# Per-head maximum and minimum subtracted ahead of two exponentials in a gated linear-attention and gMLP kernel

## The chip, the cores and the metric

The kernel runs on one core of a Trainium2 chip. The metric is the device time of one execution in microseconds. A core has five engines that work side by side, each through its own instructions in order: TensorE (PE, matmuls, with its weight loads shown as PEld), VectorE (DVE), ScalarE (ACT), GpSimd (POOL) and SyncE (SP, which here only issues DMAs). They wait for each other by semaphores.

## The reference

Two branches work on the same input `x` (2048 rows of 512 numbers) and are mixed by a gate of each row.

```python
q, k, v = heads of x @ wqkv                      # 32 heads of 16
pq, pk = q @ w_phi, k @ w_phi                    # per head, 16x16
phi_q = concat(softmax(pq), softmax(-pq))        # over the 16 of a head
phi_k = concat(softmax(pk), softmax(-pk))
kv = phi_k^T @ v ;  z = sum over rows of phi_k   # per head
a = ((phi_q @ kv) / (phi_q @ z + 1e-06)) @ wo
zz = gelu(x @ w_in) ; z1, z2 = halves, z2 layer-normalised
b = (z1 * (w_sp @ z2 + b_sp)) @ w_out
out = g * a + (1 - g) * b                        # g = sigmoid(x . gate_w)
```

The change concerns the four softmaxes: a softmax is the exponentials of 16 numbers divided by their sum, and it stays the same when one number is subtracted from all 16 beforehand.

## The kernel before, in words

The 2048 rows are 16 tiles of 128 rows (one row per partition). `xT` holds x transposed, and all weights lie in SBUF. PSUM is one tile `ps` of eight banks of 512 fp32. The order of the work is written out by hand: the scheduler is off (`tc.manual_schedule()`), so each engine gets its instructions in the order in which the program issues them, and the framework adds only the waits.

The program has three stages:

- **First stage (lines 471 to 514).** `z_piece` multiplies x by `w_in`, `z_post` applies gelu, and `bn_stats` (L224) and `ln_batch` normalise; `z1_gate` (L272) scales z1. `v_proj` (L279) makes v and `fold` (L299) multiplies the weights of q and k with `w_phi`, so that p comes out of one matmul group. At its end come `k_proj(0)`, `k_proj(1)` and then the last five `z1_gate`.
- **Key stage (lines 528 to 542).** For each tile i: `gg(1)` makes half a tile of `w_sp @ z2` (16 matmuls, L405), with the eight `kv_mm` (L377) of tile i-2 between its last matmuls; then `k_norm(i)`, then `k_proj(i+2)`. At i = 7, 9 and 11 a `q_proj` is added, and one step later another `gg(1)` and the `q_norm` that goes with it. After the loop come `q_proj(3)`, two `gg` halves, `kv_acc(15)` and `kv_extract`, which copies the masked kv out of PSUM into `kvx` (L388, L393).
- **Query stage (lines 543 to 560).** For each tile j: none to two `gg` halves (`gg_at`) with the `q_mm` (L427) of tile j, `q_num(j)` (L431: a reciprocal of the denominators and one multiply on VectorE, then a transposing DMA), `q_proj(j+4)`, `q_norm(j+3)`, and `out_tile(j-3)` (L445: ten matmuls, an eviction by ScalarE and the output's DMA, which ScalarE's queue issues).

Both `k_proj` and `q_proj` do four matmuls of 512 columns (L326) into a bank of their own pair (`KBANK`, `QBANK`) and call `feat_exp` (L331). It reads that bank twice on ScalarE: exp(p) and exp(-p), written as bf16 into a slot `e` (pieces of `w_in`, and once of `xn`, whose first content is no longer needed). `norm` (L336) then sums each 16 on VectorE (L339), takes the reciprocals (L341), and multiplies: VectorE the first half of the features, GpSimd the second (L343). `q_norm` also transposes the slot by a DMA (L371) for `q_mm`.

Each `gg` half is finished on VectorE by the step "u" (L413), which adds the bias and multiplies by z1.

Of the kernel before, what the change touches and what calls it, by code (L numbers as in the profile page):

```python
# [7 lines left out]
AF = mybir.ActivationFunctionType  # L8
ALU = mybir.AluOpType
AX = mybir.AxisListType  # L10
FP32 = mybir.dt.float32
# [3 lines left out]
P = 128  # L15
S = 2048
D = 512
H = 32
DH = 16
# [10 lines left out]
DEN_EPS = 1e-6  # L30
NHG = 8
HW = 4 * DH
# [7 lines left out]
def kernel(  # L40
# [14 lines left out]
    nc = tc.nc  # L55
# [3 lines left out]
    pers = ctx.enter_context(tc.tile_pool(name="pers", bufs=1))  # L59
    ring2 = ctx.enter_context(tc.tile_pool(name="ring2", bufs=2))  # L60
# [4 lines left out]
    ps = psp.tile([P, 8, CH], FP32, name="ps")  # L65

    def zbank(t):
# [18 lines left out]
    wphi = pers.tile([P, NDT, P], BF16, name="wphi")  # L86
    mask16 = pers.tile([P, 8], BF16, name="mask16")
    mask4 = pers.tile([P, 4], BF16, name="mask4")
    xn = pers.tile([P, 2, D], BF16, name="xn")
    ones = nc.const_aps.tensor(1.0, [P, P], BF16)  # L90
    stats = pers.tile([P, NT, 2, 6], FP32, name="stats")
# [11 lines left out]
        out=ident[:], in_=ident[:], pattern=[[-1, P]],  # L103
# [14 lines left out]
    for d0 in (0, 2):  # L118
# [6 lines left out]
        out=wv[:, :, :],  # L125
        in_=A_wqkv[:, 2 * D:3 * D].rearrange("(dt p) n -> p dt n", p=P),
    )
    for q in range(1, NCH):
        nc.sync.dma_start_transpose(
            out=xT[:, :, q * CH:(q + 1) * CH], in_=x2[q * CH:(q + 1) * CH, :]  # L130
        )
        if q == 1:
            nc.sync.dma_start(
                out=wphiW[:, :, :],
                in_=A_w_phi.rearrange("(g h) e f -> (h e) g f", g=NDT),
# [3 lines left out]
        out=bcolb[:, :, :], in_=B_b_sp.rearrange("(t p) -> t p", p=P)  # L139
# [7 lines left out]
    for t in range(WSLOTS):  # L147
        load_wsp(t)
    nc.sync.dma_start(
        out=w_out[:, 0:NFT - 1, :],  # L150
        in_=B_w_out[0:(NFT - 1) * P, :].rearrange("(ft p) n -> p ft n", p=P),
# [4 lines left out]
        out=w_out[0:last_m, NFT - 1, :], in_=B_w_out[(NFT - 1) * P:FH, :]  # L156
    )
    nc.sync.dma_start(
        out=wo[:, :, :], in_=A_wo.rearrange("(g p) n -> p g n", p=P)
# [4 lines left out]
        out=mask16[:], in_=mask16[:], pattern=[[-16, 8]],  # L164
# [3 lines left out]
        out=mask16[:], in_=mask16[:], pattern=[[16, 8]],  # L168
# [3 lines left out]
    for u in upad:  # L172
        nc.gpsimd.memset(u[:, FH:FPAD], 0.0)
    nc.gpsimd.memset(vv[:, :, :, HW:VP], 1.0)
    nc.vector.tensor_tensor(out=mask4[:], in0=mask16[:, 0:4], in1=mask16[:, 4:8], op=ALU.add)

    def z_piece(t, n0, n1, d0=0, d1=NDT):
# [136 lines left out]
    ek_t = {}  # L314
# [3 lines left out]
    def e_slot(i):  # L318
        if i == 5:
            flat = xn[:].rearrange("p t d -> p (t d)")  # L320
        else:
            flat = w_in_flat[:, i * 2 * D:(i + 1) * 2 * D]
        return flat.rearrange("p (g a n) -> p g a n", g=NHG, a=2)

    def feat_mm(t, w, b, dt):
        nc.tensor.matmul(  # L326
            ps[:, b, :], lhsT=xT[:, dt, t * P:(t + 1) * P], rhs=w[:, dt, :],
            start=(dt == 0), stop=(dt == NDT - 1),
        )

    def feat_exp(b, e):  # L331
        src = ps[:, b, :].rearrange("p (g n) -> p g n", g=NHG)
        for a, sc in enumerate((1.0, -1.0)):
            nc.scalar.activation(out=e[:, :, a, :], in_=src, func=AF.Exp, scale=sc)  # L334

    def norm(e):  # L336
        ev = e.rearrange("p g a (h f) -> p (g a h) f", h=4)
        zs = ring2.tile([P, 2 * H], FP32, name="zs")
        nc.vector.tensor_reduce(out=zs[:], in_=ev, axis=AX.X, op=ALU.add)  # L339
        rs = ring2.tile([P, 2 * H], FP32, name="rs")  # L340
        nc.vector.reciprocal(out=rs[:], in_=zs[:])  # L341
        for eng, sl in ((nc.gpsimd, slice(H, 2 * H)), (nc.vector, slice(0, H))):
            eng.tensor_tensor(  # L343
                out=ev[:, sl, :], in0=ev[:, sl, :],
                in1=rs[:, sl, None].to_broadcast([P, H, DH]), op=ALU.mult,
            )

    def k_proj(t):
        ek_t[t] = e_slot(t % 4)
        b = KBANK[t % 2]  # L350
        for dt in range(NDT):
            feat_mm(t, wk, b, dt)
        feat_exp(b, ek_t[t])

    def k_norm(t):
        norm(ek_t[t])

    def q_proj(t):
        eq_t[t] = e_slot(4 + t % 2 if t < 4 else (t - 4) % 6)
        b = QBANK[t % 2]  # L360
        for dt in range(NDT):
            feat_mm(t, wq, b, dt)
        feat_exp(b, eq_t[t])
# [2 lines left out]

    def q_norm(t):
        e = eq_t.pop(t)
        norm(e)
        eT = wqkT[:, 2 * (t % 4):2 * (t % 4) + 2, :].rearrange("p a (b n) -> p (a b) n", n=P)  # L370
        nc.sync.dma_start_transpose(out=eT, in_=e.rearrange("p g a n -> p (g a n)"))  # L371
        eT_t[t] = eT
# [14 lines left out]
    def kv_extract():  # L387
        nc.vector.tensor_tensor(  # L388
            out=kvx[:, :, 0:HW].rearrange("p g (h d) -> p g h d", h=4),
            in0=slots[:, :, 0:HW].rearrange("p g (h d) -> p g h d", h=4),  # L390
            in1=mask4[:, None, :, None].to_broadcast([P, NHG, 4, DH]), op=ALU.mult,
        )
        nc.vector.scalar_tensor_tensor(  # L393
            out=kvx[:, :, HW:QW], in0=slots[:, :, HW:HW + 1].to_broadcast([P, NHG, 4]),
            scalar=0.5 * DEN_EPS, in1=mask4[:, None, :].to_broadcast([P, NHG, 4]),
            op0=ALU.add, op1=ALU.mult,
        )

# [110 lines left out]
    for t in range(NT - VLAG, NT):  # L509
        v_proj(t)  # L510
    k_proj(0)
    k_proj(1)
    for t in range(NT - 5, NT):
        z1_gate(t)
# [13 lines left out]
    for i in range(NT):  # L528
        gg(1, kv_short(i - 2) if i >= 2 else ())
        k_norm(i)  # L530
        if i + 2 < NT:
            k_proj(i + 2)
        if i in Q_AT:
            q_proj(Q_AT[i])
        if i - 1 in Q_AT:
            gg(1)
            q_norm(Q_AT[i - 1])

    q_proj(3)
    gg(2, kv_short(NT - 2))  # L540
    kv_acc(NT - 1)
    kv_extract()
    gg_at = {0: 1, 1: 1, 2: 2, 3: 1, 5: 1, 7: 1, 9: 1, 11: 1, 13: 1, 14: 1}
    for j in range(NT):
        short = [lambda g=g: q_mm(j, g) for g in range(NHG)]
        if 0 < j and j in gg_at:
            gg(gg_at[j], short)
        else:
            gg(gg_at.get(j, 0))
            for mm in short:  # L550
                mm()
        q_num(j)
        if j + 4 < NT:
            q_proj(j + 4)
        if j + 3 < NT:
            q_norm(j + 3)
        if j >= LAG:
            out_tile(j - LAG)
# [30 lines left out]
```

## Time and profile before

| | |
|---|---|
| time, median of 3 runs | 207.92 us (207.85 to 208.15) |
| the profiled execution's own time | 208.12 us |
| its span in the profile | 206.4 us |
| busy: PE, PEld, DVE | 202.3, 117.8, 148.5 us |
| busy: ACT, POOL | 82.1, 49.5 us |
| granted TensorE clock | 1.00 |
| one feature tile on ACT (L334) | 2 x 596 ns |
| its sums, reciprocals, multiply on DVE (L339, L341, L343) | 1209, 553, 693 ns |
| its multiply on POOL (L343) | 1475 ns |
| "u" on DVE (L413) | 574 ns |
| 128x512 evictions from PSUM on ACT (L286, L457) | 603, 597 ns |

The span runs from the first to the last instruction of the profile; the rest of an execution's time lies around it. A row of a group gives its line, its engine, what it writes and reads with the shapes, the number of instructions, then their busy time and the mean of one, then the idle time of the engine just before them and what ended most of it. In a timeline the first number is the start and the second the length in microseconds, and a bracket holds the idle time before with the instruction that ended it.

### The profile page before, as it was taken

To read this page: it belongs to the slowest core of one execution; us is meant where nothing else is said; L and a number is where in the kernel's file an instruction comes from. 1 tells how busy PE (TensorE), PEld (TensorE's weight loads), DVE (VectorE), ACT (ScalarE), POOL (GpSimd) and SP (SyncE) were. 2 spreads that over 40 slices of the span, in tenths; PEclk is the share of its full clock that TensorE was granted. 3 is DMA by queue.
4 is the path that set the end of the run, shared out by engine and by line. 5 is a ranking of instruction groups with operands and counts; after the bars stand their busy time and mean duration, and the time that the engine had idled before them with its cause. 6 is when DMAs were issued, how large, how long until landed. Compare 5 with 4: busy or idle time off the path is not lost.

```text
span 206.4 us, 3685 instructions
## 1 busy us (share of the span) xinstructions
PE 202.3 (98%) x1399; PEld 117.8 (57%) x1399; DVE 148.5 (72%) x304; ACT 82.1 (40%) x145; POOL 49.5 (24%) x46
## 2 busy tenths in 40 slices
PE   8999999999999999999999999999999999999994
PEld 8545555554455666666666667666455555555542
DVE  1049858385887888879898996798989788796500
ACT  4266767675684324250505102222524243341122
POOL 4000000000002353525352543032532252322000
PEclk9999999999999999999999999999999999999999
DMA  5999899997000638463757781145756974566451
GB/s 160 289 178 247 189 170 226 168 192 231 0 3 0 140 65 117 102 112 85 153 126 109 139 174 41 38 91 84 161 131 122 127 176 98 129 141 153 110 110 51
DMA packets 90378, 26.50 MB, mean 128 GB/s; under 512 B 84296, under 2 KB 90360, under 8 KB 90360
## 3 DMA queue, kind: packets, MB, share of 16 engines
q1 hardware_dynamic: 87360, 23.87, 60.2%
q10 hardware_dynamic: 3000, 2.39, 3.8%
q8 instruction: 11, 0.18, 0.4%
q14 instruction: 7, 0.06, 0.1%
HBM read 3.44 MB, written 2.10 MB: 27 GB/s over the span
## 4 chain that ended last, share of the span: by engine, by line
PE 96%; DMA 2%; SPq 0%; ACT 0%; issue 0%
PE ps L405 36%; PE ps L180 18%; PE ps L326 13%; PE ps L448 10%; PE ps L453 7%; PE ps L282 7%; DMA w_in<-in_B_w_in_dram 2%; PE ps L427 2%; PE ps L377 2%; PE ps L305 1%; SPq L112 0%; SPq L108 0%; ACT ob L457 0%; PE ps L209 0%
## 5 line engine op out<-in xcount | busy, mean ns | idle before, releaser
L405 PE MATMUL ps<-zz,wsp 128*128 128x344 bf16 x512 | 84.1, 309 | 0.0
L343 POOL TENSOR_TENSOR w_in<-w_in,rs 128x512 bf16<-128x512 bf16 x28 | 41.3, 1475 | 124.7 <-DVE rs L341 112.4
L405 PEld LDWEIGHTS <-wsp 128*128 128x128 bf16 x512 | 49.9, 98 | 28.1
L334 ACT ACTIVATE w_in<-ps 128x512 bf16<-128x512 f32 x56 | 30.1, 596 | 63.3 <-issue 21.4
L180 PE MATMUL ps<-w_in,xT 128*128 128x512 bf16 (+2 forms) x200 | 39.7, 350 | 0.4 <-DMA w_in<-in_B_w_in_dram 0.4
L339 DVE TENSOR_REDUCE zs<-w_in 128x64 f32<-128x1024 bf16 x28 | 33.8, 1209 | 0.0
L413 DVE SCALAR_TENSOR_TENSOR u<-ps,bcol,zz 128x344 bf16<-128x344 f32 x32 | 18.4, 574 | 18.6 <-PE ps L427 8.3
L180 PEld LDWEIGHTS <-xT 128*128 128x128 bf16 x200 | 19.1, 98 | 18.0 <-issue 0.8
L215 ACT ACTIVATE zz<-ps 128x1376 bf16<-128x1376 f32 (+2 forms) x18 | 21.4, 1190 | 18.6 <-PE ps L180 18.6
L448 PE MATMUL ps<-w_out,uT 128*128 128x512 bf16 (+2 forms) x102 | 23.5, 366 | 0.0
L224 DVE BATCH_NORM_STATS2 stats<-zz 128x6 f32<-128x344 bf16 x32 | 14.8, 505 | 11.1 <-ACT zz L215 11.1
L377 PE MATMUL ps<-vv,w_in 128*128 128x65 bf16 x128 | 21.7, 193 | 0.0
L343 DVE TENSOR_TENSOR w_in<-w_in,rs 128x512 bf16<-128x512 bf16 x28 | 19.4, 693 | 1.0
L341 DVE RECIPROCAL rs<-zs 128x64 f32<-128x64 f32 x32 | 17.7, 553 | 3.2
L457 ACT ACTIVATE ob<-ps 128x512 bf16<-128x512 f32 (+2 forms) x17 | 9.7, 572 | 25.1 <-PE ps L453 19.9
L453 PE MATMUL ps<-wo,oT 128*128 128x512 bf16 (+2 forms) x68 | 16.6, 366 | 0.0
L326 PEld LDWEIGHTS <-xT 128*128 128x128 bf16 x128 | 10.8, 98 | 9.9
L326 PE MATMUL ps<-wq,xT 128*128 128x512 bf16 x64 | 16.4, 379 | 0.0
L326 PE MATMUL ps<-wk,xT 128*128 128x512 bf16 x64 | 16.3, 379 | 0.0
L427 PE MATMUL ps<-kvx,wqkT 128*128 128x68 bf16 x128 | 15.8, 194 | 0.0
L282 PE MATMUL ps<-wv,xT 128*128 128x512 bf16 x64 | 15.6, 379 | 0.0
L448 PEld LDWEIGHTS <-uT 128*128 128x128 bf16 x102 | 9.5, 98 | 10.4
(56 smaller groups left out, 134.3 us busy)
## 6 DMA issues: line engine op xcount, KB each, us to landing
out_dram<-ob ACTq DMA_DIRECT2D x15, 128.0 KB, 2.1
w_out<-in_B_w_out_dram SPq DMA_DIRECT2D x1, 640.0 KB, 4.9
w_in<-in_B_w_in_dram SPq DMA_DIRECT2D x2, 256.0 KB, 4.5
wv<-in_A_wqkv_dram SPq DMA_DIRECT2D x1, 512.0 KB, 5.0
wo<-in_A_wo_dram SPq DMA_DIRECT2D x1, 512.0 KB, 5.3
w_in<-in_B_w_in_dram SPq DMA_DIRECT2D x1, 352.0 KB, 4.9
w_in<-in_B_w_in_dram ACTq DMA_DIRECT2D x2, 128.0 KB, 4.0
w_in<-in_B_w_in_dram SPq DMA_DIRECT2D x2, 128.0 KB, 3.6
```

Source lines behind the costliest of these rows:

```text
L180: nc.tensor.matmul(zb[:, n0:n1], lhsT=xT[:, dt, t * P:(t + 1) * P], rhs=w_in[:, dt, n0:n1], start=(dt == 0), stop=(dt == NDT - 1),)
L215: nc.scalar.activation(out=zz[:, t, n0:n1], in_=zbank(t)[:, n0:n1], func=AF.Gelu_apprx_tanh)
L282: nc.tensor.matmul(ps[:, b, :], lhsT=xT[:, dt, t * P:(t + 1) * P], rhs=wv[:, dt, :], start=(dt == 0), stop=(dt == NDT - 1),)
L326: nc.tensor.matmul(ps[:, b, :], lhsT=xT[:, dt, t * P:(t + 1) * P], rhs=w[:, dt, :], start=(dt == 0), stop=(dt == NDT - 1),)
L334: nc.scalar.activation(out=e[:, :, a, :], in_=src, func=AF.Exp, scale=sc)
L339: nc.vector.tensor_reduce(out=zs[:], in_=ev, axis=AX.X, op=ALU.add)
L343: eng.tensor_tensor(out=ev[:, sl, :], in0=ev[:, sl, :], in1=rs[:, sl, None].to_broadcast([P, H, DH]), op=ALU.mult,)
L377: nc.tensor.matmul(slots[:, g, 0:HW + 1], lhsT=ek_t[t][:, g, :, :].rearrange("p a n -> p (a n)"), rhs=vv[:, t, g, 0:HW + 1], start=(t == 0 ...
L405: nc.tensor.matmul(ps[:, b, 0:HF], lhsT=wsp[:, tt % WSLOTS, s, :], rhs=zz[:, s, FH + h * HF:FH + (h + 1) * HF], start=(s == 0), stop=(s == ...
L427: nc.tensor.matmul(slots[:, g, 0:QW], lhsT=eT_t[t][:, g, :], rhs=kvx[:, g, :], start=True, stop=True)
L448: nc.tensor.matmul(ps[:, b, n0:n1], lhsT=uT[:, ft, :], rhs=w_out[:, ft, n0:n1], start=(ft == 0), stop=False,)
L453: nc.tensor.matmul(ps[:, b, n0:n1], lhsT=oT[:, g, :], rhs=wo[:, g, n0:n1], start=False, stop=(g == NDT - 1),)
```

## The change

`feat_exp` no longer reads PSUM in the exponentials. ScalarE copies the bank to SBUF as fp32, VectorE takes maximum and minimum of each head from the bank, GpSimd subtracts them from the copy (the second time in place), and the exponentials read the differences. The tiles `p32` and `top` come from a ring of two buffers. In the planned instructions of the changed kernel VectorE's maximum waits for ScalarE's copy, and GpSimd's subtractions wait for VectorE's maximum and minimum.

`norm` is split. `k_scale` is the old one. `q_scale` leaves e(p) unscaled and multiplies only e(-p), on GpSimd, by sum(e(p)) / sum(e(-p)); the common factor 1 / sum(e(p)) drops out of num / den. The small constant of the denominator goes to the first half of the features alone, by a column `epscol`.

```diff
+    epscol = pers.tile([P, 1], FP32, name="epscol")
...
+    nc.gpsimd.memset(epscol[0:HW, :], DEN_EPS)
+    nc.gpsimd.memset(epscol[HW:P, :], 0.0)
...
     def feat_exp(b, e):
-        src = ps[:, b, :].rearrange("p (g n) -> p g n", g=NHG)
+        src = ps[:, b, :].rearrange("p (h f) -> p h f", f=DH)
+        p32 = ring2.tile([P, 2, D], FP32, name="p32")
+        top = ring2.tile([P, 2, H], FP32, name="top")
+        nc.scalar.activation(out=p32[:, 1, :], in_=ps[:, b, :], func=AF.Copy)
+        for a, op in enumerate((ALU.max, ALU.min)):
+            nc.vector.tensor_reduce(out=top[:, a, :], in_=src, axis=AX.X, op=op)
         for a, sc in enumerate((1.0, -1.0)):
-            nc.scalar.activation(out=e[:, :, a, :], in_=src, func=AF.Exp, scale=sc)
-
-    def norm(e):
+            d = p32[:, a, :]
+            nc.gpsimd.tensor_tensor(
+                out=d.rearrange("p (h f) -> p h f", f=DH),
+                in0=p32[:, 1, :].rearrange("p (h f) -> p h f", f=DH),
+                in1=top[:, a, :, None].to_broadcast([P, H, DH]), op=ALU.subtract,
+            )
+            nc.scalar.activation(
+                out=e[:, :, a, :], in_=d.rearrange("p (g n) -> p g n", g=NHG),
+                func=AF.Exp, scale=sc,
+            )
+
+    def k_scale(e):
...
+    def q_scale(e):
+        zs = ring2.tile([P, 2, NHG, 4], FP32, name="zs")
+        for a in range(2):
+            nc.vector.tensor_reduce(
+                out=zs[:, a, :, :],
+                in_=e[:, :, a, :].rearrange("p g (h f) -> p g h f", h=4), axis=AX.X, op=ALU.add,
+            )
+        rs = ring2.tile([P, 2, NHG, 4], FP32, name="rs")
+        nc.vector.reciprocal(out=rs[:, 0, :, :], in_=zs[:, 1, :, :])
+        nc.vector.tensor_tensor(
+            out=rs[:, 1, :, :], in0=rs[:, 0, :, :], in1=zs[:, 0, :, :], op=ALU.mult
+        )
+        ev = e[:, :, 1, :].rearrange("p g (h f) -> p g h f", h=4)
+        nc.gpsimd.tensor_tensor(
+            out=ev, in0=ev, in1=rs[:, 1, :, :, None].to_broadcast([P, NHG, 4, DH]), op=ALU.mult,
+        )
...
     def k_norm(t):
-        norm(ek_t[t])
+        k_scale(ek_t[t])
...
     def q_norm(t):
         e = eq_t.pop(t)
-        norm(e)
+        q_scale(e)
...
         nc.vector.scalar_tensor_tensor(
             out=kvx[:, :, HW:QW], in0=slots[:, :, HW:HW + 1].to_broadcast([P, NHG, 4]),
-            scalar=0.5 * DEN_EPS, in1=mask4[:, None, :].to_broadcast([P, NHG, 4]),
+            scalar=epscol[:, 0:1], in1=mask4[:, None, :].to_broadcast([P, NHG, 4]),
```

## The prediction

> **What bounds the kernel now.** I read the page's busy table first, then the chain that ended last, then the costliest groups, then the timeline around one key tile.
>
> ```profile
> PE 202.3 (98%) x1399; PEld 117.8 (57%) x1399; DVE 148.5 (72%) x304; ACT 82.1 (40%) x145; POOL 49.5 (24%) x46
> ...
> PE 96%; DMA 2%; SPq 0%; ACT 0%; issue 0%
> ...
> L343 POOL TENSOR_TENSOR w_in<-w_in,rs 128x512 bf16<-128x512 bf16 x28 | 41.3, 1475 | 124.7 <-DVE rs L341 112.4
> ...
> L334 ACT ACTIVATE w_in<-ps 128x512 bf16<-128x512 f32 x56 | 30.1, 596 | 63.3 <-issue 21.4
> ...
> L339 DVE TENSOR_REDUCE zs<-w_in 128x64 f32<-128x1024 bf16 x28 | 33.8, 1209 | 0.0
> ```
>
> PE works without a gap and is 96% of the chain, so today the feature work costs nothing: it hides under matmuls. The stages (busy time by windows):
>
> ```profile
> 60.50:129.00 68.50, 68.50 (x539) 43.75 (x537) 57.12 (x81) 21.51 (x41) 27.88 (x19) 1.00 0.54 103
> 129.00:195.00 66.00, 66.00 (x474) 37.59 (x473) 53.19 (x84) 19.91 (x36) 19.44 (x13) 1.00 0.60 120
> ```
>
> The columns are sum, then PE, PEld, DVE, ACT, POOL. Call 60.5 to 129 the key stage and the rest the query stage. DVE is 83% busy in the key stage, so it has little room. In the chain in order of time a key tile repeats every 3.44 us (its projection starts at 79.82, 83.26). That is the pace to keep. The timeline of VectorE and of GpSimd shows two key tiles' multiplies (start, length):
>
> ```profile
> 75.34 0.69 DVE L343 TENSOR_TENSOR w_in<-w_in,rs 128x512 bf16<-128x512 bf16 x1
> 75.53 1.41 POOL L343 TENSOR_TENSOR w_in<-w_in,rs 128x512 bf16<-128x512 bf16 x1 [2.03 <-DVE rs L341]
> ...
> 78.78 0.69 DVE L343 TENSOR_TENSOR w_in<-w_in,rs 128x512 bf16<-128x512 bf16 x1
> 78.91 1.47 POOL L343 TENSOR_TENSOR w_in<-w_in,rs 128x512 bf16<-128x512 bf16 x1 [1.97 <-DVE rs L341]
> ```
>
> GpSimd's recorded start moves against VectorE's (0.19, then 0.13 us later), but its end does not: 1.60 us after VectorE's start both times, 0.91 after VectorE's end. I read this as GpSimd waiting until VectorE's multiply is done.
>
> **What the change adds.** The planned instructions confirm that it does what it says. Per 128-row tile (32 of them: 16 k, 16 q) feat_exp becomes copy (ACT), max and min (DVE, from PSUM), then subtract, exp, subtract, exp alternating over POOL and ACT. In the plan, max waits for the copy, the first subtract for max, the second for the first. ACT and POOL work in order, so the next tile's copy stands behind this tile's second exp, which stands behind its second subtract. That closes a loop from tile to tile that the old kernel lacks. Averages hide it: DVE, ACT and POOL would all still fit in the span.
>
> **Prices.**
> - Copy 0.60 (L334's 596 ns; L286 603). Exps from SBUF instead of PSUM: not shown, taken at the same 0.60; a second ACT instruction starts 0.48 after the first (a pair takes 1.08).
> - Max, min: 512 elements. L339 takes 1.21 for 1024; the PSUM-reading 128x512 rows are 0.68 (L388) and 0.75 (L435). Taken 0.68, and 0.61 back to back.
> - Subtract, 512 fp32: no fp32 row on POOL. Nearest is L343. Low end 0.91 (the part of it after VectorE is done), high end 1.47 (the whole record). Taken 1.20, the middle, because I believe the waiting but not that none of the work fits under it. The Trainium skill, "GPSIMD Engine Reference", section 3.1, gives 2.6 cycles an element at 1.2 GHz for two inputs; an estimate from it is 1.1 us for 512, and the sum below would be about 243.
> - Hand-overs: DVE to ACT/POOL and back by rows: DVE to POOL 0.15, ACT to DVE 0.03 (gelu to bn_stats), POOL to POOL 0.08 (memsets at the start), POOL to ACT not shown, 0.1.
>
> **The loop:** hand-over 0.10 + second exp until copy starts 0.48 + copy 0.60 + 0.03 + max 0.68 + 0.15 + subtract 1.20 + 0.08 + subtract 1.20 = **4.52 us** a tile, above PE's 3.44. Two neighbours sit just under it. DVE's key tile: u 0.57, reduce 1.21, reciprocal 0.55, multiply 0.69 (3.0 from start to start in the timeline) plus two reduces 1.2 = 4.2. POOL: the multiply ends 0.46 + 2.4 + 1.6 = 4.4 after the first subtract starts. So even at 0.91 a subtract, the pace stays near 4.45.
>
> **Key stage.** The key projection of tile 0 ends at 59.7; copy to 60.5, max to 61.2, subtracts 61.35 to 63.85, then tile 1 at 65.9. Its max holds up VectorE's five z1_gate steps (1.63), so tile 2's first subtract starts at 71.9. The one activation-table load (1.28) now falls between copy and exp, under the first max and subtract. Sixteen intervals follow to key tile 15: 13 at 4.52, and 3 in which q_norm of tiles 0 to 2 stands on VectorE before the next max: 0.46 + u 0.5 + q_scale 1.9 (two reduces 0.68, reciprocal 0.35 as L433, a small multiply 0.18) + u, reduce, reciprocal, multiply 3.0 + max 0.68 + 0.15 = 6.8. That is 71.9 + 58.8 + 20.4 = 151.1. Two k_norms on VectorE and POOL's last multiply take 7.45 more, 158.55. Then kv_acc, which ended at 128.98, ends at 158.85: **+29.9 us**.
>
> **Query stage.** q_mm of tile 0 follows two u's, kv_extract and a gg half, at 162.0 (131.3 before). First subtract of q4 at 164.55. The next three intervals are bound by VectorE (q_scale 1.9, q_num 1.1, max and min, one or two u's): 4.73, 5.2, 4.73. From q8 on, ACT also carries the output tile between the second exp and the next copy: eviction 0.60 and its DMA issue 0.36 (timeline rows: issue 0.34, starting 0.02 after the eviction). The interval is 4.52 + 0.96 = 5.48, eight times. First subtract of q15: 164.55 + 14.66 + 43.8 = 223.0. Then two subtracts 2.5, exp 0.7, reduce, reciprocal, small multiply 1.3, POOL 1.35, the transpose's landing 3.2 (page, DMA issues): q_mm of tile 15 at 232.1. Before, it started at 194.5 to 194.6 and the span ended 11.8 later, PE-bound; that tail is unchanged: 243.9. PE needs 63.1 us between q_mm of tiles 0 and 15 and gets 70, so it isn't the bound there.
>
> What is removed hides under this: the q tiles' VectorE multiply (0.69 x 16), which was off the path. kv_extract's scalar becomes a column and two memsets are added at the start: nothing, POOL is idle until 65; bounds 0 to 0.2 us.
>
> The profiled run took 208.12 for a span of 206.4, so 1.72 lies around it (median of the runs shown: 207.92, 0.2 less, within what they scatter). 243.9 + 1.7 = 245.6: **246 us, 18% slower**. With subtracts at 0.91: key stage at its floor, query intervals 4.9, together 7 less, 239. At 1.47: 13 x 0.55 + 8 x 0.55 + 3 at the ends = 14 more, 260.
>
> **Rivals.**
> 1. GpSimd's 1.47 is all work, and the constant end only a trait of its records (the page calls POOL's spans rough). Loop 5.07; 260. For it: both multiplies have the same releaser, so a constant end proves no wait. Against: then the start should not wander by 0.09 while the end stays. 25%.
> 2. POOL gets in first. Its second subtract runs late, takes VectorE's multiply from the front, and VectorE waits through a GpSimd multiply. This needs the second subtract to end later than 2.85 after the first started (mine: 2.48), so subtracts above 1.38 or jitter. Then 1.2 + 0.69 + 0.68 + 0.15 follow instead: 5.5 a key tile, 13 x 1.0 more: 259. The Trainium skill, "SBUF — State Buffer", section "SBUF: two separate sides", states such a rule: VectorE with two SBUF inputs and a reading GpSimd instruction exclude each other for a whole instruction, whoever starts first. The constant end above agrees with it, and it speaks against this change, which triples POOL's instructions. 10%.
> 3. Not slower: the loop stays under PE's 3.44 and everything hides as before, 208. It decides at 2.12 fixed + two subtracts = 3.44, so 0.66 a subtract. The row's smallest reading is 0.91, and VectorE's 4.2 a key tile stands against it as well. For it: no engine's total exceeds the span (DVE about 180, POOL about 126). 2%.
> 4. fp32 doubles GpSimd's price, or PE's granted clock (1.00 now) falls in its new gaps: over 268. 5%.
>
> **How the numbers follow.** Forecast 58% (239 to 252 its own range); rivals as above. The range 237 to 266 takes in both ends of the subtract and rivals 1 and 2. About 0.2% (0.4 us) can be told from no change; same and faster each have 1%, from rival 3.
>
> **What would show it.** POOL about 0.55 to 0.6 busy; subtract 1.0 to 1.3 us; key tiles 4.5 us apart; PE idle in the key stage, released by POOL or DVE; in the chain, ACT copy, DVE max and POOL subtract following each other; the 11.8 us tail unchanged. Wrong if max doesn't wait for the copy in the trace, or if POOL's waits are on VectorE's reciprocal alone.

## The result, and the profile after

The changed kernel takes **243.30 us** (median of 3, 242.98 to 243.62) against 207.92: 1.170 times, interval 1.167 to 1.173. The forecast was 246 in a range of 237 to 266. The profiled execution took 243.62, its span is 241.8, 35.4 more than before.

The page after, in the order of the lines shown of before (busy table, chain by engine and by line, groups):

```profile
PE 210.1 (87%) x1376; PEld 118.4 (49%) x1399; DVE 177.9 (74%) x384; ACT 104.0 (43%) x177; POOL 110.1 (46%) x112
...
PE 34%; DVE 28%; POOL 19%; issue 9%; ACT 6%; DMA 2%; ACTq 2%; DVEq 0%; POOLq 0%
...
L343 POOL TENSOR_TENSOR p<-p,top 128x512 f32<-128x512 f32 x64 | 67.7, 1058 | 90.4 <-DVE top L340 87.8
...
L340 DVE TENSOR_REDUCE top<-ps 128x32 f32<-128x512 f32 x64 | 41.2, 685 | 20.1 <-ACT p L338 19.9
...
L360 POOL TENSOR_TENSOR w_in<-w_in,rs 128x512 bf16<-128x512 bf16 x16 | 23.6, 1477 | 16.5 <-DVE rs L358 15.5
```

No engine is over 87% busy, yet the kernel is 17% slower. The chain, which was 96% PE, is now split among four engines. L340's idle time says where VectorE waits: for ScalarE's copy, 19.9 us.

The query stage shows the loop link by link. This is the chain in order of time for one interval (start, length, engine, line; pieces called issue are hand-overs):

```profile
190.35 0.61 ACT p L338
...
191.05 0.70 DVE top L340
...
191.82 0.57 POOL p L343
192.39 0.53 issue
192.96 1.07 POOL p L343
...
194.58 0.59 ACT ob L491
195.19 0.34 ACTq L492
...
195.63 0.61 ACT p L338
```

Copy, maximum, two subtractions (the first cut in two by the profile), the wait of about 0.5 in which the second exp occupies ScalarE, the output eviction, its DMA issue, and the next copy: 5.28 us, then the same again. All eight such intervals measure 5.28 to 5.33.

By stage (windows 60.5 to 129; sum, then PE, PEld, DVE, ACT, POOL, then the granted clock), VectorE's share is as before while PE has lost 14 us:

```profile
60.50:129.00 68.50, 54.15 (x358) 31.06 (x363) 56.92 (x88) 26.61 (x45) 48.48 (x42) 0.93 0.36 68
```

### The profile page after: what moved, and what is told of

The parts are those of the page before. It is cut to its first block, busy times and chain, and to the rows that moved or that the text cites. A ratio compares the mean times of both kernels' runs of the same rounds, so it can differ in the third digit from the quotient of the medians.

```text
span 241.8 us, 3913 instructions
## 1 busy us (share of the span) xinstructions
PE 210.1 (87%) x1376; PEld 118.4 (49%) x1399; DVE 177.9 (74%) x384; ACT 104.0 (43%) x177; POOL 110.1 (46%) x112
## 4 chain that ended last, share of the span: by engine, by line
PE 34%; DVE 28%; POOL 19%; issue 9%; ACT 6%; DMA 2%; ACTq 2%; DVEq 0%; POOLq 0%
PE ps L183 15%; POOL p L343 14%; DVE top L340 9%; PE ps L285 6%; PE ps L439 5%; DVE zs L356 5%; POOL w_in L360 4%; DVE u L447 3%; DVE rs L358 3%; PE ps L482 3%; ACT p L338 3%; DVE zs L368 2%; DMA w_in<-in_B_w_in_dram 2%; PE ps L487 2%; ACT ob L491 2%
## 5 line engine op out<-in xcount | busy, mean ns | idle before, releaser
L343 POOL TENSOR_TENSOR p<-p,top 128x512 f32<-128x512 f32 x64 | 67.7, 1058 | 90.4 <-DVE top L340 87.8
L439 PE MATMUL ps<-zz,wsp 128*128 128x344 bf16 x512 | 91.2, 318 | 14.5 <-DVE u L447 14.5
L439 PEld LDWEIGHTS <-wsp 128*128 128x128 bf16 x512 | 51.1, 100 | 46.8 <-issue 17.9
L348 ACT ACTIVATE w_in<-p 128x512 bf16<-128x512 f32 x56 | 35.3, 630 | 80.0 <-POOL p L343 80.0
L340 DVE TENSOR_REDUCE top<-ps 128x32 f32<-128x512 f32 x64 | 41.2, 685 | 20.1 <-ACT p L338 19.9
L360 POOL TENSOR_TENSOR w_in<-w_in,rs 128x512 bf16<-128x512 bf16 x16 | 23.6, 1477 | 16.5 <-DVE rs L358 15.5
L411 PE MATMUL ps<-vv,w_in 128*128 128x65 bf16 x128 | 23.1, 200 | 5.2 <-DVE w_in L360 4.5
L338 ACT ACTIVATE p<-ps 128x512 f32<-128x512 f32 x32 | 18.8, 586 | 6.0 <-PE ps L329 2.2
L356 DVE TENSOR_REDUCE zs<-w_in 128x64 f32<-128x1024 bf16 x16 | 19.3, 1208 | 0.0
L411 PEld LDWEIGHTS <-w_in 128*128 128x128 bf16 x128 | 11.9, 102 | 10.0 <-DVE w_in L360 5.7
```

The costliest lines, as they stand in the source:

```text
L338: nc.scalar.activation(out=p32[:, 1, :], in_=ps[:, b, :], func=AF.Copy)
L340: nc.vector.tensor_reduce(out=top[:, a, :], in_=src, axis=AX.X, op=op)
L343: nc.gpsimd.tensor_tensor(out=d.rearrange("p (h f) -> p h f", f=DH), in0=p32[:, 1, :].rearrange("p (h f) -> p h f", f=DH), in1=top[:, a, : ...
L348: nc.scalar.activation(out=e[:, :, a, :], in_=d.rearrange("p (g n) -> p g n", g=NHG), func=AF.Exp, scale=sc,)
L360: eng.tensor_tensor(out=ev[:, sl, :], in0=ev[:, sl, :], in1=rs[:, sl, None].to_broadcast([P, H, DH]), op=ALU.mult,)
L411: nc.tensor.matmul(slots[:, g, 0:HW + 1], lhsT=ek_t[t][:, g, :, :].rearrange("p a n -> p (a n)"), rhs=vv[:, t, g, 0:HW + 1], start=(t == 0 ...
```

## The experiments

**Minimum and second subtraction, one at a time and together.** Three kernels. In all three the shift that is left out would have cancelled in the softmax. The loop theory says that there are two nearly equal bounds in the key stage; its rivals, that VectorE's or GpSimd's amount of work alone sets the pace.

```diff
-        for a, op in enumerate((ALU.max, ALU.min)):
-            nc.vector.tensor_reduce(out=top[:, a, :], in_=src, axis=AX.X, op=op)
+        nc.vector.tensor_reduce(out=top[:, 0, :], in_=src, axis=AX.X, op=ALU.max)
...
-                in1=top[:, a, :, None].to_broadcast([P, H, DH]), op=ALU.subtract,
+                in1=top[:, 0, :, None].to_broadcast([P, H, DH]), op=ALU.subtract,
```

> Leaves out the 32 minimum reductions; both subtractions take the maximum. The minimum is not on the tile-to-tile loop (copy, maximum, subtract, subtract, exp, next copy), but it is 0.60 us of VectorE's work a tile. Loop theory (two nearly equal bounds, loop about 4.2 and VectorE 4.2 in the key stage, loop alone in the query stage): key intervals stay at 4.2, the three long ones fall from 6.5 to 5.9, the output-tile intervals of the query stage stay at 5.29; about 6 us off, 237. Rival, VectorE's work alone sets the pace: 0.6 off in some 29 intervals, 17 us, 226.

Measured 238.97 us, 4.3 off. The ordinary key intervals (from one tile's first subtraction to the next one's) are 4.21 or 4.22, all alike, where the changed kernel mostly alternates between 4.21 and 4.39. The query intervals stay at 5.29. The three long ones fall to 6.11, not to 5.9. So 4.21 is the loop by itself, and VectorE alone isn't the bound.

```diff
-            nc.gpsimd.tensor_tensor(
...
+            if a == 0:
+                nc.gpsimd.tensor_tensor(
...
```

> Leaves out the second subtraction on GpSimd; exp(-p) reads the unsubtracted copy. Loop theory: the loop loses 1.1 and gains the second exp's 0.54, about 3.6 in the key stage, so VectorE's 4.2 holds there (0.1 off in 13 intervals, the long ones unchanged); in the query stage 5.29 falls to VectorE's mean of about 4.8. Together some 6 us off, 237. Rival, GpSimd's total work sets the pace: 32 x 1.06 off, 34 us, 209.

Measured 234.07, 9.2 off, more than expected: key intervals 4.19, query intervals 4.67 and not 4.8, and where a q tile follows a k tile at once the interval fell to 3.59, which I had not counted. GpSimd's work as the bound (209) is out.

> Leaves out both the minimum and the second subtraction. If loop and VectorE are two nearly equal bounds, taking both away gives more than the two single gains together: key intervals fall to about 3.6 (PE's own 3.44 next), 0.65 x 13; the long ones to 5.9; query intervals to about 4.65; some 20 us off, 223 to 224, against 12 for the sum of the single ones. If one bound alone sets the pace, the gain equals the larger single one plus little.

Measured 223.99, 19.3 off, where the single ones give 4.3 + 9.2 = 13.5. Key intervals are 3.59 and 3.79. Two bounds side by side: taking one away shows only a part of it.

**The loop cut, all work kept.** ScalarE gets the next tile's copy ahead of this tile's exps, so no copy stands behind a subtraction.

```diff
+    def exps():
+        while late:
+            p32, e = late.pop()
+            for a, sc in enumerate((1.0, -1.0)):
+                nc.scalar.activation(
...
         nc.scalar.activation(out=p32[:, 1, :], in_=ps[:, b, :], func=AF.Copy)
+        exps()
...
-            nc.scalar.activation(
-                out=e[:, :, a, :], in_=d.rearrange("p (g n) -> p g n", g=NHG),
-                func=AF.Exp, scale=sc,
-            )
+        late.append((p32, e))
```

`exps()` issues the exps of the tile before. Where no projection follows, it is called by itself.

> All work kept; only ScalarE's order changes: the copy of the next tile is issued ahead of the two exps of this one, so that no copy stands behind a GpSimd subtraction. Loop theory: query intervals fall from 5.29 to VectorE's mean of about 4.75 (8 x 0.5), key intervals to VectorE's 4.2 (13 x 0.1), and the second tile's maximum no longer waits at the start (about 3 us): 8 us off, 235. Rivals: if VectorE or GpSimd set the pace everywhere, the query intervals stay at 5.29 and only the start gains, 240.

Measured **224.55 us** (1.078 times the kernel before, 1.076 to 1.081): 18.75 off, more than twice what I expected. VectorE's waits for the copy (us in total, times, longest) in the changed kernel and here:

```profile
DVE top L340 <- ACT p L338: 19.9, 15, 3.1
```

```profile
DVE top L352 <- ACT p L349: 0.8, 2, 0.5
```

The key intervals are 4.19, the query intervals 4.12 and 4.60 in turn. The same window of the key stage:

```profile
60.50:129.00 68.50, 59.40 (x434) 35.26 (x433) 66.78 (x102) 32.14 (x52) 55.98 (x49) 1.00 0.43 82
```

VectorE is busy 66.78 of 68.5, so it is now the bound. Some 3.3 us of this is not work but time in which its instructions stood beside GpSimd's (the five z1_gate 3.69 instead of 1.63, and three multiplies 1.14, 1.07 and 1.07 instead of 0.69; both come back below). My expectation took VectorE's work per interval as if each were a key tile. But a q tile that follows a k tile gives VectorE only 1.3 us to do, and there the loop held it for 3.1 us (the longest of its waits for the copy). VectorE does all three tiles of such a group in 12.24 us instead of the loop's 15.1; the three groups give 8.6 of the 18.75 us, the eight query intervals 7.5.

**z1_gate ahead of the first key tiles.**

```diff
-    k_proj(0)
-    k_proj(1)
     for t in range(NT - 5, NT):
         z1_gate(t)
+    k_proj(0)
+    k_proj(1)
```

> All work kept: copies ahead of the exps, and the last five z1_gate steps moved ahead of the first two key projections on VectorE. In the changed kernel they took 2.88 us beside GpSimd's subtractions, 1.63 before. Theory (they wait for GpSimd's subtractions): they take 1.63 again, the first key tiles come up to 1.3 us earlier than with the copies moved alone. Rival (they are slow for another reason, or off the path): the same time as with the copies moved alone.

Measured 222.85, 1.7 off the version with the copies moved alone. The timeline of VectorE, in the changed kernel, with the copies moved alone, and here:

```profile
66.16 2.88 DVE L275 TENSOR_SCALAR zz<-zz,st 128x688 bf16<-128x688 bf16 x5
```

```profile
62.40 3.69 DVE L275 TENSOR_SCALAR zz<-zz,st 128x688 bf16<-128x688 bf16 x5
```

```profile
60.03 1.63 DVE L275 TENSOR_SCALAR zz<-zz,st 128x688 bf16<-128x688 bf16 x5
```

The same five instructions take 1.25 us longer while GpSimd subtracts twice, and 2.06 longer beside a row of four subtractions. In the changed kernel the longest of the five is recorded at 1215 ns, the median at 386.

**VectorE or GpSimd, once the loop is cut.** Both kernels start from the last one (222.85).

> The version with copies first and z1_gate first (222.85), the minimum left out, both subtractions with the maximum. VectorE theory (with the loop cut, VectorE's work is the whole rest): 0.6 off a tile, key intervals 4.19 to about 3.7 where GpSimd's 2.2 + 1.4 comes next; 11 to 13 us off, 210 to 212. GpSimd theory (its 110 us are the rest): no change, 222 to 223.

Measured 211.62: 11.2 off, as VectorE's theory says. Key intervals are 3.62.

> The same version with the second subtraction left out and the minimum kept. VectorE theory: no change, 222 to 223, since GpSimd isn't the bound. GpSimd theory: 1.06 off a tile, 210 or less.

Measured 220.59, 2.3 off. The key and query intervals are unchanged (4.19; 4.12 and 4.60). Part of the gain lies at the start and where two subtraction pairs follow each other. There GpSimd holds up VectorE's multiply: with four subtractions in a row (VectorE's and GpSimd's timelines)

```profile
101.72 1.14 DVE L368 TENSOR_TENSOR w_in<-w_in,rs 128x512 bf16<-128x512 bf16 x1
```

```profile
97.97 4.34 POOL L354 TENSOR_TENSOR p<-p,top 128x512 f32<-128x512 f32 x4
```

it ends 0.55 us after the last subtraction, and with two of the four left out it takes its usual time:

```profile
100.65 0.69 DVE L368 TENSOR_TENSOR w_in<-w_in,rs 128x512 bf16<-128x512 bf16 x1
```

This happens three times (1.14, 1.08 and 1.08). So GpSimd's amount of work is not the bound, but where its instructions run into VectorE's it still costs VectorE time.

**All three together.**

> Copies ahead of the exps, the five z1_gate steps first, no minimum, one subtraction: the loop is cut and VectorE has 3.6 us a key tile, GpSimd 2.6. If loop and VectorE's work are the whole cause, PE's 3.44 is nearly the bound again: key intervals 3.6, long ones under 6, query intervals at PE's mean of 4.44, a start some 5 us late; 212 to 214. Rival (something else costs, such as the longer way from the matmul to the finished feature): 218 or more.

Measured **208.95**, 1.005 times the kernel before (1.003 to 1.007), better than expected. The page:

```profile
PE 201.3 (97%) x1376; PEld 117.8 (57%) x1399; DVE 156.7 (76%) x352; ACT 101.5 (49%) x177; POOL 75.8 (37%) x80
```

PE is the bound again, with ScalarE's 32 copies, VectorE's 32 maxima and GpSimd's 32 subtractions under it. So the loop, VectorE's work and the time in which GpSimd holds VectorE up make up all but 1 us of the cost; that last 1 us was not followed further.

**The output's DMA issue taken from ScalarE.**

```diff
-            out_part(t, (2, 6)[t % 2], 0, D, ob, nc.scalar)
+            out_part(t, (2, 6)[t % 2], 0, D, ob, nc.sync)
```

> The changed kernel, with the output tiles' DMAs issued by SyncE's queue instead of ScalarE's. The forecast counted eviction and DMA issue as links of the query-stage loop. Theory: the issue and its hand-overs (0.4 to 0.45 us) leave eight intervals, 5.29 becomes 4.85, about 3.4 us off, 240. Rival (the issue runs beside, the loop is bound elsewhere): no change.

Measured 238.86, 4.4 off. The query intervals fall to 4.70, by 0.59. ScalarE's timeline there:

```profile
192.70 0.58 ACT L491 ACTIVATE ob<-ps 128x512 bf16<-128x512 f32 x1
193.18 0.59 ACT L338 ACTIVATE p<-ps 128x512 f32<-128x512 f32 x1
```

The copy now starts 0.48 after the eviction; in the changed kernel it started 1.05 after (194.58, 195.63). The issue costs more than its own 0.34 because it waits until the eviction has ended, and ScalarE can't start the copy meanwhile.

**What GpSimd's 1.47 us was.** The kernel before, without VectorE's half of the multiply:

```diff
-        for eng, sl in ((nc.gpsimd, slice(H, 2 * H)), (nc.vector, slice(0, H))):
+        for eng, sl in ((nc.gpsimd, slice(H, 2 * H)),):
```

> The kernel before with VectorE's half of the multiply left out (the first half of the features stays unscaled). If GpSimd's 1.47 us was mostly waiting for VectorE's multiply, its records shrink to about 1.06; if it was all work, they stay at 1.47. The time stays at 207.9 in both, PE-bound.

Measured 207.96 (1.0006, 0.9996 to 1.0016). The group:

```profile
L343 POOL TENSOR_TENSOR w_in<-w_in,rs 128x512 bf16<-128x512 bf16 x28 | 29.6, 1057 | 136.1 <-DVE rs L341 122.7
```

1057 ns instead of 1475: it was waiting. (The first 512 features are left unscaled here.) The changed kernel holds a case that I had not planned, a multiply that starts late, here in VectorE's and GpSimd's timelines:

```profile
101.65 0.69 DVE L360 TENSOR_TENSOR w_in<-w_in,rs 128x512 bf16<-128x512 bf16 x1
```

```profile
102.09 1.17 POOL L360 TENSOR_TENSOR w_in<-w_in,rs 128x512 bf16<-128x512 bf16 x1 [1.06 <-DVE rs L358]
```

It starts 0.44 after VectorE's and is recorded at 1.17; it ends 0.92 after VectorE's end, where all others end 0.90 to 0.92 after it. Of the 1.06 of work some 0.14 fits under the wait.

**The parts alone.** First the query scaling with the old exponentials, then the subtraction with the old scaling.

> One part alone: the exponentials read PSUM as in the kernel before, and only the query scaling (q_scale and the column epscol) is taken from the change. It takes 0.69 us of multiply a query tile off VectorE and adds nearly nothing; PE is the bound there. Theory (off the path): 207.9, within 0.4. Rival (VectorE's relief lets PE run closer): 1 us faster or more.

Measured 208.07 (1.0011, 0.9999 to 1.0023): nothing that can be told.

> The other part alone: subtraction as in the change, but query tiles scaled as the kernel before does (reduce, reciprocal, a multiply on VectorE and on GpSimd each, and the constant's half as before). Theory (VectorE binds the three long key intervals and the first query intervals, the loop the rest): 0.6 more in six intervals and some in the tail, about 247. Rival (q_scale is the cause of part of the slowdown): below 243.

Measured 247.92. The three long key intervals are 7.14 to 7.21 (6.50 to 6.58 in the changed kernel), the first query intervals 5.24 and 5.65 (4.60 and 5.02), the later ones 5.28 to 5.33 in both. So the new scaling earns 4.6 us inside the change, only where VectorE is the bound.

## Why the prediction was right, point by point

- **The bound moves to a loop across ScalarE, VectorE and GpSimd, not to a full engine: right.** Cutting it by ScalarE's order alone gives back 18.75 of 35.4 us. The rest by steps: z1_gate's place 1.7, the minimum on VectorE 11.2, the second subtraction 2.7, and 1.0 is left. The steps depend on their order: the minimum alone, with the loop in place, was worth 4.3. Of the signs named, GpSimd's share was too high: 46%, not 55 to 60%.
- **The subtraction, taken at 1.20: 1.06.** This is the largest mis-sized term, 0.28 a tile. The loop is 4.21 and not 4.52. The reading that GpSimd waits for VectorE was right (rival 1 falls: the alternative price gave 260).
- **The floor of 4.45 under the key stage: too high.** It came from the end of GpSimd's multiply, and that sum held two subtractions at 1.20; at the 0.91 for which the floor was named it gives 3.9, so VectorE's 4.2 was the floor. The 13 ordinary key intervals average 4.32 (4.21 to 4.58); the three long ones 6.53, forecast 6.8 (the terms listed for them add up to 6.7). `kv_acc` ends at 156.1, forecast 158.85.
- **VectorE at 4.2 a key tile: right**, 4.19 in the kernel with the loop cut. Having it so near the loop is why no single removal gave much.
- **The start: forecast 71.9 for tile 2's first subtraction, measured 72.84.** I moved z1_gate but priced it at its old 1.63; beside the subtractions it took 2.88.
- **The query stage: eight intervals of 5.48, measured 5.29**, each link as listed. First subtraction of q15 at 218.25, forecast 223.0.
- **The tail: wrong step, small.** From that subtraction to q_mm of tile 15 I counted 9.1 us through exp, multiply and transpose; it took 11.65. The chain there is PE's own (`gg` halves and two output tiles) from the q_mm of tile 13 at 221.74, which waited for q_num. By the median landing time of 3.2 the transpose was there about 2 us earlier. The stretch behind it was unchanged, as forecast: 11.9 us in both kernels.
- **Part of the nearness is luck.** The first subtraction of q15 came 4.75 us earlier than forecast and the tail took 2.55 longer. The two misses partly cancel in 246 against 243.3.
- **"What is removed hides under this": true of the kernel before, not of the change.** The query multiply is off the path there (208.07 without it), but with the subtraction in place its absence earns 4.6 us.
- **Rival 2 (GpSimd gets in first) did not happen**: the second subtraction ends 2.19 after the first one's start, below the 2.85 needed. VectorE's multiply stays 0.69 throughout the changed kernel. With the loop cut a milder form does appear: three of its multiplies wait for a running subtraction (1.07 to 1.14). The rule behind it holds all the same: the Trainium skill, "SBUF — State Buffer", section "SBUF: two separate sides", says that such a pair excludes each other for a whole instruction; here 1.06 alone, and an end tied to VectorE's with any start. It calls the blocking full, and 0.14 of 1.06 ran under it.
- **The Trainium skill's price was nearer than mine**: the Trainium skill, "GPSIMD Engine Reference", section 3.1, gives 2.6 cycles an element, an estimate of 1.1 us; measured 1.058.
- **Rival 4 did not happen as a cost**: fp32 didn't double GpSimd's price (1058 ns), and the clock did fall, without a visible price; see below.

## What to carry to other kernels

Where each tile's work hops between engines that run in order, write down the loop from one tile's first step to the next one's; its length can set the pace though no engine is full. Here it was broken without extra work, by issuing the next tile's first step ahead of this tile's last. When two bounds are close, remove both before judging either. A record that always ends at the same distance from another engine's instruction holds waiting, and its length is no price.

## What the runs showed of the hardware that I had not expected

- GpSimd's two-input instruction on 128x512 takes 1058 ns in fp32 (L343) and 1058 in bf16 (L378), with an fp32 second input in both: the type made no difference here.
- VectorE's one-input bf16 scaling is held up by GpSimd too (five z1_gate 1.63 alone, 2.88 and, with the copies moved, 3.69 beside subtractions), while its reductions kept their length: 1201 to 1210 ns for the sums (1206 to 1210 before), 680 to 693 for the maximum and minimum.
- The granted TensorE clock fell after two of PE's idle gaps. PE had no matmul for 5.53 us up to 108.48, and the clock was 0.50 from 107 to 113; after 2.42 us without one (up to 123.58) it was 0.50 from 124 to 127; 3.20 us without one (up to 138.69) left it at 1.00. No rule comes out of these three. Windows of the changed kernel from 100, 105 and 110 us (PE is the number after the sum, the clock the third from the end):

```profile
100.00:105.00 5.00, 2.95 (x19) 1.76 (x18) 3.43 (x5) 2.29 (x4) 3.86 (x4) 1.00 0.72 120
105.00:110.00 5.00, 1.52 (x6) 0.82 (x6) 3.31 (x5) 2.09 (x4) 2.52 (x3) 0.67 0.13 29
110.00:115.00 5.00, 4.95 (x26) 2.67 (x26) 4.89 (x11) 2.43 (x5) 4.05 (x4) 0.65 0.20 39
```

PE was not the bound there: the three groups of a k, a q and a k tile from 103.22, 118.32 and 133.42 take 15.10 us each, the first two with the low clock in them, the third at 1.00. In the profiled run with only ScalarE's order changed, where PE's gaps from 60 us on are 2.11 us at most, the clock is 1.00.
